# Three small reorderings in a fused attention and feed-forward kernel: batch 0's second chunk squared earlier, a matmul between two means, the last copy on two engines

## The chip, the cores and the metric

The kernel runs on one core of one Trainium2 chip. Times are device microseconds (us). Each profile is one execution; its span is 1.7 to 2.1 us shorter than the measured time of the same execution. Before the change the time was 284.89 us, the median of three runs (284.84 to 284.98).

## The reference

```python
def _attn_ref(q, k, v, g_norm):                    # (8, 8, 576, 64)
    kv = np.einsum('bhsd,bhse->bhde', k, v)
    out = np.einsum('bhsd,bhde->bhse', q, kv)
    rms = np.sqrt(np.mean(out * out, axis=-1, keepdims=True) + 1e-06)
    return out / rms * g_norm
# x = out, transposed to (4608 tokens, 512)
def _moe_ref(x, w_in, w_out):                      # 512 -> 2048 -> 512
    h = x @ w_in
    g = np.where(h > 0.0, h, np.exp(np.minimum(h, 0.0)) - 1.0)
    return g @ w_out
```

## The kernel before

Tokens are worked in tiles of 512. For the first tile, x is built in four chunks of 128 features (0, 2, 1, 3), and the first matmuls with `w_in` start as soon as a chunk is normalized. `idle` matmuls on zeros fill the start. The second tile (batch 1) is built in two groups, between the `mm2` matmuls (`o_ps`) of the first one. The parts that the change and the argument touch:

```python
def chunk_y(c, ps): ...            # y of chunk c: TensorE, 64-wide
def chunk_square(c):               # ScalarE
    nc.scalar.activation(sq0[c], y_ps[c], AF.Square)
def inv_t(r, ps):                  # ScalarE: Ln, then Exp(-0.5 *)
    nc.scalar.activation(r, ps, AF.Ln, bias=eps_col)
    nc.scalar.activation(r, r, AF.Exp, scale=-0.5)
# ... start of the kernel (cut) ...
    mean_mm(sq0[2], mean)
    inv_t(r[:, 1, :], mean)                     # chunk 2: Ln, Exp
    ...
    chunk_kv(kv_ps, 3)                          # needs chunk 3's v
    chunk_kv_out(kv_ps, 3, V)
    chunk_y(1, single("m", "y_ps"))
    chunk_square(1)
    ...
    chunk_y(3, y3)
    chunk_square(3)
    chunk_scale(2, r[:, 1, :])
    early([(0, 0), (0, 1)], 0)                  # matmuls of chunk 0
    mean_mm(sq0[1], mean)
    nc.scalar.activation(r[:, 0, :], mean, AF.Ln, bias=eps_col)
# ... a group of tile 1 (cut) ...
        for l in range(2):
            n.sums(l, single("m", "mean"))      # one mean matmul
            n.inv(l); n.scale(l)                # ScalarE, VectorE
        mm2_all(*((7, 11), (13, 15))[u])
# ... the last 128 tokens, 256 columns at a time (cut) ...
        for n, eng in enumerate((A, V)):        # ScalarE, then VectorE
            ...
            copy_on(eng, o, ps)
            last_store(J - 1, o, cols)
```

Of the kernel before, what the change touches and what calls it, by code (L numbers as in the profile page):

```python
# [10 lines left out]
AF = mybir.ActivationFunctionType  # L11
# [5 lines left out]
def kernel(  # L17
# [13 lines left out]
    nc = tc.nc  # L31
    P = 128

    B, H, S, D = q.shape
# [8 lines left out]
    V, A, Q = nc.vector, nc.scalar, nc.gpsimd  # L43
# [20 lines left out]
    eps_col = const.tile([P, 1], FP32, name="eps_col")  # L64
# [43 lines left out]
    def copy_on(eng, out_, in_):  # L108
        if eng is nc.scalar:
            nc.scalar.copy(out_, in_)  # L110
        else:
            eng.tensor_copy(out=out_, in_=in_)  # L112
# [16 lines left out]
    def single(tag, name):  # L129
        pool = ps_x if tag == "x" else ps_m2  # L130
        return pool.tile([P, 512], FP32, name=name, tag=tag)

    def pair(tag, name):
        if tag in ("x", "m", "mx"):
            return [single(t, name) for t in (tag + tag)[:2]]
        return ps_m1.tile([P, 2, 512], FP32, name=name, tag=tag)

    def as_bf16(ps):
        return ps.bitcast(BF16)
# [11 lines left out]
    def kv_mm(b, kv_ps, u, ls=range(2)):  # L151
        for j in range(RK):
            for s in range(2):
                rows = slice(s * 64, s * 64 + 64)
                for l in ls:
                    nc.tensor.matmul(  # L156
                        kv_ps[s][l * 64 : l * 64 + 64, u * 64 : u * 64 + 64],
                        lhsT=bf["k", b][rows, 2 * l + u, j, :],
                        rhs=bf["v", b][rows, 2 * l + u, j, :],
                        start=(j == 0),  # L160
                        stop=(j == RK - 1),
                    )

    def kv_out(b, kv_ps, u, engs):
        for s in range(2):
            copy_on(engs[s], kv_sb[:, b, u, s], kv_ps[s][:, u * 64 : u * 64 + 64])
# [11 lines left out]
    def q_t_out(b, u, eng, src, js):  # L178
        copy_on(eng, qT[b][:, :, u, js, :], src.rearrange("p (j s r) -> p s j r", s=2, r=64))

    def y_mm(T, u, ps, ls=range(2)):

        n = 0
        while n < 8:
            b, j = slot_of(T, n)
            m = min(8 - n, RK - j)
            for l in ls:
                for s in range(2):
                    nc.tensor.matmul(  # L189
                        ps[l][s * 64 : s * 64 + 64, n * 64 : (n + m) * 64],  # L190
                        lhsT=kv_of(b, l, u, s),
                        rhs=qT[b][l * 64 : l * 64 + 64, s, u, j : j + m, :],
                        start=True,
                        stop=True,
                    )
            n += m

    def mean_mm(sq, ps):
        nc.tensor.matmul(ps, lhsT=ones, rhs=sq, start=True, stop=True)  # L199
# [4 lines left out]
    def r_tile():  # L204
        return outp.tile([P, 2, G], FP32, name="rT", tag="o")

    def inv_t(r, ps):
        nc.scalar.activation(r, ps, AF.Ln, bias=eps_col)
        nc.scalar.activation(r, r, AF.Exp, scale=-0.5)  # L209

    def scale_t(T, ps, r, cs, cols=slice(0, 512)):
        nc.vector.scalar_tensor_tensor(  # L212
            out=xT[T][:, cs, cols], in0=ps, scalar=g_col, in1=r, op0=ALU.mult, op1=ALU.mult
        )
# [208 lines left out]
    def last_store(j, o, cols):  # L423
        rows = out_dram.rearrange("(b p j) f -> b p j f", b=B, j=RK)
        for h, eng in enumerate((nc.scalar, nc.sync)):
            b, jj = slot_of(NT - 1, 2 * j + h)
            eng.dma_start(out=rows[b][:, jj, cols], in_=o[h * 64 : h * 64 + 64])
# [5 lines left out]

    def last_columns():

        for n, eng in enumerate((A, V)):
            cols = slice(n * 256, n * 256 + 256)
            ps = single("m", "o_ps")[:, 0:256]
            for f in range(FC):
                nc.tensor.matmul(  # L440
                    ps,
                    lhsT=gT[NT - 1][:, f, (J - 1) * P : J * P],
                    rhs=w_out_sb[:, f, cols],
                    start=(f == 0),
                    stop=(f == FC - 1),
                )
            o = outp.tile([P, 2, DM], FP32, name="o_sb", tag="o")[:, 0, 0:256]
            copy_on(eng, o, ps)
            last_store(J - 1, o, cols)

    def mm2_half(T, i):
# [71 lines left out]
    def idle(n, ps):  # L523
        for _ in range(n):
            nc.tensor.matmul(ps, lhsT=zeros[:, 0:P], rhs=zeros, start=True, stop=True)

    def turned_q(b, u, tag):

        ps = as_bf16(single(tag, "qt_ps"))
        q_t_mm(b, u, range(8), ps)  # L530
        return ps
# [4 lines left out]
    def chunk_kv(kv_ps, c):  # L536
        kv_mm(0, [kv_ps[:, s, :] for s in range(2)], c % 2, (c // 2,))

    def chunk_kv_out(kv_ps, c, eng):
        rows, cols = slice(c // 2 * 64, c // 2 * 64 + 64), slice(c % 2 * 64, c % 2 * 64 + 64)  # L540
        copy_on(eng, kv_sb[rows, 0, c % 2], kv_ps[rows, :, cols])

    y_ps, sq0 = {}, {}

    def chunk_y(c, ps):
        y_ps[c] = ps
        y_mm(0, c % 2, {c // 2: ps}, (c // 2,))

    def chunk_square(c):
        sq0[c] = attp.tile([P, G], BF16, name="sq", tag="sq")  # L550
        nc.scalar.activation(sq0[c], y_ps[c], AF.Square)

    def chunk_scale(c, r, cols=slice(0, 512)):
        scale_t(0, y_ps[c][:, cols], r[:, cols], c, cols)
# [10 lines left out]
    def early(tiles, c):  # L565

        for i, a in tiles:
            h = h_ps[i]
            nc.tensor.matmul(  # L569
                h[a] if isinstance(h, list) else h[:, a, :],  # L570
                lhsT=w_in_sb[:, c, (2 * i + a) * P : (2 * i + a) * P + P],
                rhs=xT[0][:, c, :],
                start=(c == 0),
                stop=(c == KC - 1),
            )
# [10 lines left out]
    ps = turned_q(0, 0, "m")  # L586
# [5 lines left out]
    mean = pair("A", "mean")[:, 0, :]  # L592
# [10 lines left out]
    mean_mm(sq0[0], mean)  # L603
    r = r_tile()
    inv_t(r[:, 0, :], mean)
    mean = single("m", "mean")
    ps = turned_q(0, 1, "m")
    q_t_out(0, 1, V, ps, slice(0, 8))
    mean_mm(sq0[2], mean)
    inv_t(r[:, 1, :], mean)  # L610
    kv_ps = pair("B", "kv_ps")
    h_ps = [pair("A", "h_ps")]
    chunk_kv(kv_ps, 1)
    chunk_kv_out(kv_ps, 1, V)
    idle(2, h_ps[0][:, 0, :])
    chunk_scale(0, r[:, 0, :])
    chunk_kv(kv_ps, 3)
    chunk_kv_out(kv_ps, 3, V)
    chunk_y(1, single("m", "y_ps"))
    chunk_square(1)  # L620
    idle(1, h_ps[0][:, 0, :])
    y3 = single("x", "y_ps")
    h_ps += [None, [single("x", "h_ps"), None]]
    chunk_y(3, y3)
    chunk_square(3)
    chunk_scale(2, r[:, 1, :])
    h_ps[1] = pair("B", "h_ps")
    early([(0, 0), (0, 1)], 0)
    mean = single("m", "mean")
    mean_mm(sq0[1], mean)  # L630
    r = r_tile()
    nc.scalar.activation(r[:, 0, :], mean, AF.Ln, bias=eps_col)
    early([(1, 0), (1, 1), (2, 0)], 0)
    for n in range(2):
        cols = slice(n * 256, n * 256 + 256)
# [20 lines left out]
    def mm2_all(f0, f1, js=range(4)):  # L656
        for f in range(f0, f1):
            for j in js:
                mm2(0, j, f, f + 1)

    for tag, j0 in (("A", 0), ("B", 2)):
        ps = pair(tag, "o_ps")
# [4 lines left out]
    for u in range(2):  # L667
        n = Turned(1, u)
        if u == 0:
            for js in ((0, 1), (2, 3)):  # L670
                mm2_all(0, 4, js)
        kv_ps = [single("x", "kv_ps") for _ in range(2)]
        kv_mm(1, kv_ps, u)
        kv_out(1, kv_ps, u, (A, A))
        main = turned_q(1, u, "m")
        q_t_out(1, u, V, main, slice(0, 8))
        ends = as_bf16(single("m", "qt_ps"))
        for t in range(2):
            q_t_mm(t, u, (8,), ends[:, t * P : t * P + P])
        for t in range(2):  # L680
            q_t_out(t, u, V, ends[:, t * P : t * P + P], slice(8, 9))
        mm2_all(*((4, 6), (11, 12))[u])
        n.product([single("x", "y_ps") for _ in range(2)])
        for l in range(2):
            n.square(l)
        mm2_all(*((6, 7), (12, 13))[u])
        for l in range(2):
            n.sums(l, single("m", "mean"))
            n.inv(l)
            n.scale(l)  # L690
        mm2_all(*((7, 11), (13, 15))[u])
    for js in ((2, 3), (0, 1)):
        for j in js:
            mm2(0, j, 15, 16, out=False)
# [29 lines left out]
    ps = pair("B", "h_ps")  # L724
# [13 lines left out]
    ps = pair("A", "o_ps")  # L738
# [30 lines left out]
    for T in range(2, NT):  # L769
        at, early, late = {}, {}, {}  # L770
        if T + 1 < NT:
# [12 lines left out]
            early = {2: ("sum0", "inv0"), 4: ("sum1", "inv1"), 5: ("gain0",), 7: ("gain1",)}  # L784
            late = {0: ("kv",), 1: ("se0",), 2: ("mul0",), 3: ("se1",), 4: ("mul1", "ahead")}
        if T == 2:
            early = {2: ("sum0", "inv0"), 5: ("sum1", "inv1", "mul1"), 6: ("gain0",), 7: ("gain1",)}
# [45 lines left out]
```

## Time and profile before

| | before |
|---|---|
| time, median of 3 | 284.89 us |
| span of the profile | 283.0 us |
| TensorE busy | 273.8 us, 97% |
| chain of waits: TensorE's share | 93% |
| last matmul's end to last copy's end | 0.52 us |

What this bounds, and the lines that carry it, are in the prediction. In the timeline, start and length come first, then engine, source line, operation, output and inputs, and in brackets the idle time ahead of the first instruction of the row with what ended it. This is GpSimd in the profile of before, at the first piece of work that waits for batch 4's q:

```profile
60.61 4.07 POOL L103 CAST q_bf<-st_q 128x384 bf16<-128x384 f32 x6 [5.40 <-DMA st_q<-in_q_dram]
```

The bracket says that GpSimd sat idle until that load had landed, so 60.6 is the landing. And this is VectorE some 8 us later, with the transposes of x by DMA that it waits for:

```profile
69.02 0.48 DVE L312 TENSOR_SCALAR xT<-xT,g_col 128x1024 bf16<-128x1024 bf16 x1
70.70 0.48 DVE L312 TENSOR_SCALAR xT<-xT,g_col 128x1024 bf16<-128x1024 bf16 x1 [1.20 <-DMA xT<-xs]
```

The second of these ended at 71.18. TensorE came to its first matmul on it at 71.30 and did not have to wait.

### The profile page before, as it was taken

To read this page: it belongs to the slowest core of one execution; us is meant where nothing else is said; L and a number is where in the kernel's file an instruction comes from. 1 tells how busy PE (TensorE), PEld (TensorE's weight loads), DVE (VectorE), ACT (ScalarE), POOL (GpSimd) and SP (SyncE) were. 2 spreads that over 40 slices of the span, in tenths; PEclk is the share of its full clock that TensorE was granted. 3 is DMA by queue.
4 is the path that set the end of the run, shared out by engine and by line. 5 is a ranking of instruction groups with operands and counts; after the bars stand their busy time and mean duration, and the time that the engine had idled before them with its cause. 6 is when DMAs were issued, how large, how long until landed. Compare 5 with 4: busy or idle time off the path is not lost.

```text
span 283.0 us, 5120 instructions
## 1 busy us (share of the span) xinstructions
PE 273.8 (97%) x2089; PEld 128.9 (46%) x2123; DVE 164.9 (58%) x222; ACT 141.6 (50%) x209; POOL 50.0 (18%) x89
## 2 busy tenths in 40 slices
PE   7799999999999999999999999999999999999994
PEld 3444444444544444444444444444444444444443
DVE  2549532867578647655775478537873786344600
ACT  3778359594667355425542555245533553333311
POOL 7743303341340033034003210000000000000000
PEclk9999999999999999999999999999999999999999
DMA  7999999999996979689528961602150235020222
GB/s 209 201 204 206 206 263 228 208 257 180 199 264 89 155 210 223 80 211 249 140 30 175 263 159 39 162 17 74 39 111 0 74 39 111 0 76 0 74 74 75
DMA packets 50571, 39.46 MB, mean 139 GB/s; under 512 B 30964, under 2 KB 44020, under 8 KB 50548
## 3 DMA queue, kind: packets, MB, share of 16 engines
q0 software_dynamic: 15008, 21.30, 37.6%
q1 hardware_dynamic: 35136, 17.31, 28.6%
q10 hardware_dynamic: 404, 0.53, 0.5%
q8 instruction: 16, 0.26, 0.4%
q14 instruction: 7, 0.06, 0.1%
HBM read 36.70 MB, written 9.44 MB: 163 GB/s over the span
## 4 chain that ended last, share of the span: by engine, by line
PE 93%; DMA 3%; POOL 1%; issue 1%; DVE 1%; ACT 0%; POOLq 0%; DVEq 0%
PE o_ps L403 43%; PE h_ps L382 42%; DMA v_bf<-in_v_dram 3%; PE at L250 2%; PE at L156 2%; PE h_ps L569 1%; PE o_ps L440 1%; POOL k_bf L90 1%; PE mean L199 0%; PE qt_ps L174 0%; PE kv_ps L156 0%; PE y_ps L189 0%; POOL v_bf L90 0%; DVE xT L212 0%; POOL q_bf L90 0%
## 5 line engine op out<-in xcount | busy, mean ns | idle before, releaser
L403 PE MATMUL o_ps<-w_out_sb,gT 128*128 128x512 bf16 x548 | 128.4, 379 | 0.7 <-issue 0.2
L382 PE MATMUL h_ps<-xT,w_in_sb 128*128 128x512 bf16 (+1 forms) x540 | 126.4, 376 | 1.0
L350 ACT ACTIVATE elu_e<-h_ps 128x1024 bf16<-128x1024 f32 (+1 forms) x79 | 74.1, 952 | 89.2 <-PE h_ps L382 78.4
L403 PEld LDWEIGHTS <-gT 128*128 128x128 bf16 x560 | 54.3, 98 | 65.9 <-issue 0.9
L366 DVE TENSOR_TENSOR gT<-elu_e,h_ps 128x1024 bf16<-128x1024 bf16 (+1 forms) x67 | 77.2, 1157 | 6.9 <-PE h_ps L382 0.5
L382 PEld LDWEIGHTS <-w_in_sb 128*128 128x128 bf16 x560 | 53.2, 98 | 61.1 <-issue 0.2
L362 DVE TENSOR_SCALAR elu_e<-elu_e 128x1024 bf16<-128x1024 bf16 x72 | 31.5, 437 | 64.5 <-ACT elu_e L350 64.4
L419 ACT COPY o_sb<-o_ps 128x512 f32<-128x512 f32 x32 | 18.4, 588 | 20.8 <-PE o_ps L403 20.1
L103 POOL CAST q_bf<-st_q 128x384 bf16<-128x384 f32 x36 | 18.5, 558 | 38.0 <-DMA st_q<-in_q_dram 32.9
L283 DVE TENSOR_REDUCE ss<-sq 128x16 f32<-128x1024 bf16 x14 | 17.1, 1218 | 6.5 <-ACT sq L277 6.5
L299 DVE TENSOR_TENSOR xs<-at,ss 128x1024 bf16<-128x1024 f32 x14 | 17.1, 1219 | 1.9 <-ACT ss L292 1.9
L277 ACT ACTIVATE sq<-at 128x1024 bf16<-128x1024 f32 x14 | 14.4, 1028 | 0.0
L212 DVE SCALAR_TENSOR_TENSOR xT<-y_ps,g_col,rT 128x512 bf16<-128x512 f32 (+1 forms) x10 | 6.2, 641 | 10.1 <-ACT rT L209 7.9
L339 POOL COPY gate<-qT 1x16 bf16<-1x16 bf16 x5 | 1.1, 217 | 58.9 <-DMA qT<-q_bf 58.9
L355 ACT ACTIVATE elu_h<-h_ps 128x1024 bf16<-128x1024 f32 (+1 forms) x12 | 9.3, 816 | 0.0
L156 PEld LDWEIGHTS <-k_bf 64*64 64x64 bf16 x576 | 6.4, 107 | 5.5 <-issue 5.5
L90 POOL DMA_DIRECT2D v_bf<-in_v_dram x11 | 7.8, 711 | 4.2 <-DMA w_in_sb<-in_moe_w_in_dram 2.1
L90 POOL DMA_DIRECT2D k_bf<-in_k_dram x11 | 7.7, 702 | 2.5 <-DMA w_in_sb<-in_moe_w_in_dram 1.7
L312 DVE TENSOR_SCALAR xT<-xT,g_col 128x1024 bf16<-128x1024 bf16 x14 | 6.7, 480 | 1.9 <-DMA xT<-xs 1.9
L366 DVE TENSOR_TENSOR gT<-elu_e,elu_h 128x1024 bf16<-128x1024 bf16 x9 | 6.6, 736 | 0.8
L250 PEld LDWEIGHTS <-qT 64*128 64x128 bf16 (+1 forms) x248 | 4.3, 97 | 6.1 <-issue 5.9
L112 DVE COPY o_sb<-o_ps 128x256 f32<-128x256 f32 x1 | 0.4, 425 | 11.1 <-PE o_ps L440 11.1
(57 smaller groups left out, 100.4 us busy)
## 6 DMA issues: line engine op xcount, KB each, us to landing
st_q<-in_q_dram POOLq DMA_DIRECT2D x6, 1152.0 KB, 8.0
out_dram<-o_sb SPq DMA_DIRECT2D x24, 256.0 KB, 3.4
k_bf<-in_k_dram POOLq DMA_DIRECT2D x6, 576.0 KB, 10.2
v_bf<-in_v_dram POOLq DMA_DIRECT2D x6, 576.0 KB, 12.4
out_dram<-o_sb SPq DMA_DIRECT2D x19, 128.0 KB, 2.4
w_out_sb<-in_moe_w_out_dram POOLq DMA_DIRECT2D x4, 512.0 KB, 15.5
w_in_sb<-in_moe_w_in_dram POOLq DMA_DIRECT2D x2, 512.0 KB, 10.7
q_bf<-in_q_dram POOLq DMA_DIRECT2D x3, 288.0 KB, 13.5
```

The source lines that it names most:

```text
L90: eng.dma_start(out=dst.rearrange("p m j d -> p m (j d)"), in_=in_[:, ms, :])
L103: nc.gpsimd.tensor_copy(out=bf["q", b][:, u, js], in_=raw[b][:, u::2, js, :].rearrange("p l j d -> p j l d"),)
L156: nc.tensor.matmul(kv_ps[s][l * 64 : l * 64 + 64, u * 64 : u * 64 + 64], lhsT=bf["k", b][rows, 2 * l + u, j, :], rhs=bf["v", b][rows, 2 * ...
L277: nc.scalar.activation(sq, st["se", h], AF.Square)
L283: nc.vector.reduce_sum(out=ss, in_=st.pop(("sq", h)).rearrange("p l (m e) -> p (l m) e", e=D), axis=AX.X,)
L299: nc.vector.tensor_tensor(out=st["xs"][:, 2 * h : 2 * h + 2, :].rearrange("p i (l m e) -> p l i m e", l=2, e=D), in0=se_ps.rearrange("p l ...
L350: nc.scalar.activation(e[:, lo:hi, :], h, AF.Exp)
L362: nc.vector.tensor_scalar(out=e, in0=e, scalar1=1.0, scalar2=1.0, op0=ALU.min, op1=ALU.subtract)
L366: nc.vector.tensor_tensor(out=gT[T][:, 2 * i + lo : 2 * i + hi, :], in0=e[:, lo:hi, :], in1=h, op=ALU.add if relu else ALU.max,)
L382: nc.tensor.matmul((ps[a] if isinstance(ps, list) else ps[:, a, :])[:, cols], lhsT=w_in_sb[:, c, f * P : f * P + P], rhs=xT[T][:, c, cols] ...
L403: nc.tensor.matmul(o_ps[T, j], lhsT=gT[T][:, f, j * P : j * P + P], rhs=w_out_sb[:, f, :], start=(f == 0), stop=(f == FC - 1),)
L419: nc.scalar.copy(o_sb[T, half][:, j % 2, :], o_ps[T, j])
```

## The change

The intent: chunk 1 of the first tile is ready earlier (part 1); no idle time stands between the two means of a group (part 2); each of two engines copies only half of the last 256 columns (part 3).

```diff
@@ part 1 @@
-    mean = single("m", "mean")
     ps = turned_q(0, 1, "m")
     q_t_out(0, 1, V, ps, slice(0, 8))
+    mean = single("m", "mean")
     mean_mm(sq0[2], mean)
-    inv_t(r[:, 1, :], mean)
+    nc.scalar.activation(r[:, 1, :], mean, AF.Ln, bias=eps_col)
 ...
     chunk_scale(0, r[:, 0, :])
+    chunk_y(1, single("m", "y_ps"))
+    chunk_square(1)
+    nc.scalar.activation(r[:, 1, :], r[:, 1, :], AF.Exp, scale=-0.5)
     chunk_kv(kv_ps, 3)
     chunk_kv_out(kv_ps, 3, V)
-    chunk_y(1, single("m", "y_ps"))
-    chunk_square(1)
 ...
     chunk_y(3, y3)
-    chunk_square(3)
     chunk_scale(2, r[:, 1, :])
-    h_ps[1] = pair("B", "h_ps")
-    early([(0, 0), (0, 1)], 0)
 ...  (mean and Ln of chunk 1)
+    chunk_square(3)
+    h_ps[1] = pair("B", "h_ps")
+    early([(0, 0), (0, 1)], 0)
@@ part 2 @@
+        f0, f1 = ((7, 11), (13, 15))[u]
         for l in range(2):
             n.sums(l, single("m", "mean"))
             n.inv(l)
             n.scale(l)
-        mm2_all(*((7, 11), (13, 15))[u])
+            mm2_all(f0, f0 + 1, ((0,), (1, 2, 3))[l])
+        mm2_all(f0 + 1, f1)
@@ part 3 @@
-            copy_on(eng, o, ps)
+            if n == 0:
+                nc.scalar.copy(o, ps)
+            else:
+                nc.scalar.copy(o[:, 0:128], ps[:, 0:128])
+                nc.vector.tensor_copy(out=o[:, 128:256], in_=ps[:, 128:256])
```

More of the change, by code (lines that the diff above doesn't have):

```diff
@@ L434, in last_columns @@
     def last_columns():
-        for n, eng in enumerate((A, V)):
+        for n in range(2):
             cols = slice(n * 256, n * 256 + 256)
```

## The prediction

> **What bounds the kernel now.** I read the page of the profile first, then the chain that ended last (whole, and piece by piece for the first 45 us), then the timeline in narrow windows around the three places that the diff touches, and the landings of the loads that feed them.
>
> From the page, the span, the busy shares and the chain by engine:
>
> ```profile
> span 283.0 us, 5120 instructions
> PE 273.8 (97%) x2089; PEld 128.9 (46%) x2123; DVE 164.9 (58%) x222; ACT 141.6 (50%) x209; POOL 50.0 (18%) x89
> PE 93%; DMA 3%; POOL 1%; issue 1%; DVE 1%; ACT 0%; POOLq 0%; DVEq 0%
> ```
>
> TensorE is the bound nearly everywhere, so only a gap on TensorE, or work before its first or after its last matmul, can be won. The measured time is 284.89 us, 1.9 over the span. The change touches gaps of tenths of a microsecond: everything below is in hundredths.
>
> **First place, 12 to 18 us.** The chain there, start and length in us:
>
> ```profile
> 4.96 7.08 DMA v_bf<-in_v_dram
> ...
> 12.69 0.30 DVE kv_sb L112
> ...
> 13.09 0.40 PE y_ps L189 x2
> 13.49 0.54 PE h_ps L569 x2
> 14.03 0.23 PE mean L199
> 14.26 0.02 issue
> 14.29 0.70 ACT rT L632
> ...
> 15.01 0.43 ACT rT L636
> ...
> 15.86 0.49 DVE xT L212
> ```
>
> Four chunks of x are normalized in the order 0, 2, 1, 3. The early matmuls use chunk 0, then 2, and wait for chunk 1: the last of chunk 2 starts at 15.81, a matmul takes a slot of 0.216, so TensorE is free at 16.03 and starts chunk 1 at 16.39. That gap is 0.36. Chunk 3 starts at 17.71, where it could have started at 17.68. After that TensorE runs without a gap for many microseconds, so **what counts is when chunk 3 is ready**, not the larger gap before it.
>
> **Second place, 34 to 47 us**, batch 1's two groups. The timeline of group 1 (start, length, engine):
>
> ```profile
> 42.32 1.04 PE L403 MATMUL o_ps<-w_out_sb,gT 128*128 128x512 bf16 x4
> 43.19 0.74 PE L199 MATMUL mean<-sq,ones 128*128 128x512 bf16 x2
> 43.77 0.38 PE L403 MATMUL o_ps<-w_out_sb,gT 128*128 128x512 bf16 x1
> 46.23 0.75 DVE L212 SCALAR_TENSOR_TENSOR xT<-y_ps,g_col,rT 128x512 bf16<-128x512 f32 x1 [0.49 <-ACT rT L209]
> 46.79 1.48 PE L382 MATMUL h_ps<-xT,w_in_sb 128*128 128x512 bf16 x6
> ```
>
> The two means start at 43.19 and 43.56, 0.365 apart where 0.216 would do: the second waits for ScalarE's second square (42.92 to 43.51). So 0.15 of TensorE time is lost; group 0 shows the same (35.79 and 36.16). But look at the last two lines. The last chunk of x for tile 1 is ready at 46.98, and TensorE, which arrives at 47.01, starts it at 47.04. **The ScalarE/VectorE chain from the first mean to that chunk (43.19 to 46.98) and TensorE's own work between are within 0.03 of each other.** A gap filled between them buys nothing unless the first mean itself moves.
>
> What can hold the first mean? The four o_ps matmuls ahead of it read the last quarter of w_out. Its load:
>
> ```profile
> 27.45 0.77 POOL L122 DMA_DIRECT2D w_out_sb<-in_moe_w_out_dram  x1 [0.73 <-DMA k_bf<-in_k_dram]
> DMA to landing us min/median/max: 14.7/14.7/14.7
> ```
>
> It lands at about 42.10 (27.45 + 14.7, rounded in the view), 0.22 before its first use at 42.32. The DMA engines are full here, so it will not land sooner.
>
> **Third place, the end**:
>
> ```profile
> 277.42 0.37 ACT L110 COPY o_sb<-o_ps 128x256 f32<-128x256 f32 x1 [1.16 <-PE o_ps L440]
> 279.22 0.42 DVE L112 COPY o_sb<-o_ps 128x256 f32<-128x256 f32 x1 [11.10 <-PE o_ps L440]
> 279.68 0.47 SPq L427 DMA_DIRECT2D out_dram<-o_sb  x1
> 279.68 0.50 ACTq L427 DMA_DIRECT2D out_dram<-o_sb  x1
> ```
>
> The last matmul ends at 279.13, VectorE copies 279.22 to 279.65, the two stores go out at 279.68. All of this is on the path to the end.
>
> [...] the built order of the changed kernel shows the dependency: VectorE's half waits for a ScalarE count that is exactly that of ScalarE's half, where before it waited for TensorE. **The two halves run one after the other.** [...] squares of 512 take 0.60, Ln with its bias 0.69, and two squares start 0.50 apart. [...] from a 128-wide matmul to a 64-wide weight load passes 0.31 instead of 0.216.
>
> **The change, part by part.**
>
> (1) Chunk 1 ahead of chunk 3. No instruction is added or removed. I rebuild the stretch with the durations above. The idle matmul before chunk 1's product starts at 11.57, so the product starts at 11.88 (mode change 0.31) and ends at 12.28; its square runs 12.32 to 12.92 (ScalarE waits 0.24 for it), and chunk 2's Exp 12.82 to 13.45. Chunk 3's v lands at 12.04 as before, its product starts at 13.03 to 13.09. The mean of chunk 1 follows at 13.37 instead of 13.87, since two h matmuls no longer stand before it; its Ln starts at 13.80 instead of 14.29. But chunk 3's square now stands between Ln and Exp: 14.39, and the Exp's first half starts at 14.89 instead of 15.01. Gain 0.12, passed on by the scale to chunk 1 (16.27). Chunk 3: its mean at 15.10, Ln at 15.52 instead of 15.63, its last half scaled by 17.55, first matmul at 17.60 instead of 17.71. **Sum: 0.11 won**, not 0.36, because ScalarE still does the same four instructions before chunk 1's Exp.
>
> (2) A matmul between the means. In group 0 the 0.15 is filled: TensorE reaches group 1 0.11 + 0.15 = 0.26 earlier. The w_out quarter's first use would be at 42.06, but it lands at 42.10, and a matmul released by another engine starts some 0.05 after it (16.33 to 16.39 above): 42.15. So 0.17 of the 0.26 survives. In group 1 TensorE fills the second 0.15, but then arrives at the last chunk of x at 46.69, and that chunk is ready 0.17 earlier than before, not 0.32: it waits till 46.87. **Sum of (1) and (2): 0.17 won**, and group 1's filled gap comes back as a wait of 0.17. If (1) gave nothing, (2) alone would give 0.15 or 0.16.
>
> (3) The shared copy. ScalarE starts some 0.04 after the last matmul (as at 277.42): 279.17. 128 columns cost 0.373 - 128/1.2 ns = 0.27: ends 279.43. VectorE starts 0.03 later (its usual distance from ScalarE, 46.20 to 46.23) and takes 0.425 - 128/0.96 ns = 0.29: ends 279.76, instead of 279.65. **0.11 lost.** The stores are unchanged.
>
> Sum: 284.89 - 0.17 + 0.11 = **284.83 us**.
>
> **Rivals.** (A) The filled gaps count in full: 0.11 + 0.15 + 0.15 = 0.41 won, 0.11 lost, 284.59. For it: TensorE is 97% busy. Against it: the last chunk's readiness within 0.03 of TensorE's arrival. (B) The halves of the copy overlap: 0.13 won at the end instead of 0.11 lost, 284.59 with my 0.17. For it: two engines, half the columns. Against it: the wait in the built order. (C) The reordered start loses: ScalarE's wait of 0.24 for chunk 1's product, or the square before the Exp, pushes chunk 3 out by 0.1 to 0.2. Then the group 1 gate still has slack to take it, 0.0 to 0.1 won in all, 284.9 to 285.0. (D) The w_out quarter lands later in a run: less won, 284.9.
>
> **Range and chances.** The runs of before lie within 0.14 of each other. A and B mark the low side and C and D the high side, neither likely beyond 0.25: range 284.60 to 285.05. Two per cent is 5.7 us, which no part comes near: faster 0.01, same 0.98, slower 0.01.
>
> **What would show it.** In the changed profile: chunk 3's early matmuls start near 17.60; group 0's means stand 0.43 apart with an o_ps matmul between and no gap; the first matmul with the last w_out quarter starts 0.1 to 0.2 earlier than 42.32, not 0.26; a new TensorE gap of some 0.17 stands before the fourth h_ps matmul of tile 1; at the end a ScalarE copy of 128x128, then, not beside it, a VectorE copy, and stores some 0.6 us after the last matmul instead of 0.55. The prediction is wrong if the stretch 10 to 18 us moves by more than 0.2 either way, if tile 1's fourth matmul moves by 0.3, or if the two copies overlap.

Three figures need what the profile of before measured beside them. The "mode change" is the step from a 128-wide matmul to a 64-wide weight load, 0.309 us (34.26 to 34.57). "Full" means that from 27.45 to 42.10 us the DMA engines were busy for 90% or more of each of 40 slices, at 228 GB/s; that the load will not land sooner was an estimate. And the columns a ns in part (3), 1.2 and 0.96, are what two lengths in that profile give: ScalarE's copies of `o_ps` took 0.588 us for 512 columns and 0.373 for 256, so 1.19 columns a ns, and VectorE's products of `y_ps` 0.748 and 0.480, so 0.96.

## The result, and the profile after

The changed kernel takes 285.20 us (285.00 to 285.85, six runs), against 284.94 (284.82 to 285.59, six runs) for the kernel before in the same rounds. A ratio is the mean time of one kernel's fast runs over that of the other's of the same rounds, so it is not quite the ratio of these medians: here 1.0007, with a 95% interval of 0.9993 to 1.0021. That is "the same", as predicted, but the median lies 0.15 above the predicted range.

From the page of the changed kernel, the span, the busy times and the chain's shares:

```profile
span 283.3 us, 5120 instructions
PE 274.8 (97%) x2089; PEld 129.5 (46%) x2123; DVE 164.3 (58%) x222; ACT 141.4 (50%) x210; POOL 49.9 (18%) x89
PE 96%; DVE 1%; issue 1%; ACT 1%
```

TensorE has the same matmuls and is busy 1.0 us longer. Of that, 0.67 shows in the timeline of TensorE's first microseconds, in the ten idle matmuls. First before, then after:

```profile
1.19 3.78 PE L525 MATMUL kv_ps<-zeros 128*128 128x512 bf16 x10 [1.19 <-DVE one L518]
```

```profile
1.19 4.45 PE L529 MATMUL kv_ps<-zeros 128*128 128x512 bf16 x10 [1.19 <-DVE one L522]
```

The same ten matmuls took 3.78 and 4.45 us. The profile's clock record of TensorE rises to full speed at 4.15 us in the one and at 6.73 in the other; below it a slot (from the start of one 512-column matmul to that of the next) is 0.427 us, above it 0.216. The change does not touch anything there. In the twenty profiles the rise lies between 4.15 and 7.17 us, 3.02 apart, in kernels whose starts differ at most by two idle matmuls and one memset of a single number. What sets the moment was not shown.

**The first place.** The chain of the changed kernel, start and length, at its beginning and at this stage:

```profile
1.19 4.44 PE kv_ps L529 x10
5.64 0.19 PE g_ps L586
```

```profile
13.79 0.34 PE mean L199
14.12 0.02 issue
14.15 0.69 ACT rT L634
14.83 0.49 ACT sq L555
15.32 0.32 ACT rT L641
15.63 0.02 issue
15.66 0.34 DVE xT L212
16.00 0.06 issue
16.06 0.48 DVE xT L212
16.55 0.04 issue
16.59 0.59 PE h_ps L573 x2
```

As predicted, chunk 3's square (L555) stands between chunk 1's Ln and Exp. But the chain now comes from the ten idle matmuls, where before it came from the load of v (the prediction shows it), and the first Ln starts at 10.58 instead of 10.16. Chunk 3's first matmul starts at 17.97, not at the predicted 17.60; before, it was 17.71.

**The second place.** The timeline of TensorE in group 1, and the chain right behind it:

```profile
42.43 1.04 PE L403 MATMUL o_ps<-w_out_sb,gT 128*128 128x512 bf16 x4
43.30 0.38 PE L199 MATMUL mean<-sq,ones 128*128 128x512 bf16 x1
43.52 0.38 PE L403 MATMUL o_ps<-w_out_sb,gT 128*128 128x512 bf16 x1
43.74 0.38 PE L199 MATMUL mean<-sq,ones 128*128 128x512 bf16 x1
```

```profile
46.49 0.65 PE h_ps L382 x3
47.14 0.01 issue
47.15 1.02 PE h_ps L382 x4
```

The gap between the means is filled: 43.30, 43.52, 43.74 are 0.216 apart. The fourth h_ps matmul comes 0.386 after the third (46.76 to 47.15) where a slot is 0.216: 0.17 of waiting, the size that the prediction gave. But the first matmul on the last quarter of w_out starts at 42.43, later than before (42.32), not earlier. The trace counts that quarter as landed at 42.23; before, at 42.10. In neither profile did the landing hold it: TensorE got there 0.20 and 0.22 after it. The 0.11 is chunk 3's delay of 0.26 less the 0.15 that was filled in group 0.

**The third place**, the end:

```profile
279.35 0.27 ACT L451 COPY o_sb<-o_ps 128x128 f32<-128x128 f32 x1 [1.38 <-PE o_ps L440]
279.64 0.29 DVE L452 COPY o_sb<-o_ps 128x128 f32<-128x128 f32 x1 [11.34 <-ACT o_sb L451]
279.96 0.47 SPq L427 DMA_DIRECT2D out_dram<-o_sb  x1
```

VectorE's half waits for ScalarE's half, as predicted. The last copy ends 0.626 after the last matmul, before 0.517: **0.109 lost, predicted 0.11**.

The difference of the spans (283.27 less 282.96, so 0.31) is then: 0.11 at the end of tile 1 (TensorE gets there at 52.97 instead of 52.86), 0.07 around 71 us (VectorE's second multiplication starts at 71.05 instead of 70.70), 0.11 at the end, and 0.02 in the closing instructions. Only the last but one is plainly the change. The experiments had to show whether any of the rest is.

### The profile page after: what moved, and what is told of

The parts are those of the page before. It is cut to its first block, busy times and chain, and to the rows that moved or that the text cites. A ratio compares the mean times of both kernels' runs of the same rounds, so it can differ in the third digit from the quotient of the medians.

```text
span 283.3 us, 5120 instructions
## 1 busy us (share of the span) xinstructions
PE 274.8 (97%) x2089; PEld 129.5 (46%) x2123; DVE 164.3 (58%) x222; ACT 141.4 (50%) x210; POOL 49.9 (18%) x89
## 4 chain that ended last, share of the span: by engine, by line
PE 96%; DVE 1%; issue 1%; ACT 1%
PE o_ps L403 43%; PE h_ps L382 42%; PE at L250 2%; PE kv_ps L529 2%; PE at L156 2%; PE o_ps L440 1%; PE h_ps L573 1%; PE qt_ps L174 1%; PE kv_ps L156 1%; PE mean L199 1%; PE y_ps L189 1%; DVE kv_sb L112 0%; DVE xT L212 0%; DVE qT L112 0%; ACT rT L634 0%
## 5 line engine op out<-in xcount | busy, mean ns | idle before, releaser
L350 ACT ACTIVATE elu_e<-h_ps 128x1024 bf16<-128x1024 f32 (+1 forms) x79 | 74.0, 952 | 89.4 <-PE h_ps L382 78.6
L362 DVE TENSOR_SCALAR elu_e<-elu_e 128x1024 bf16<-128x1024 bf16 x72 | 30.9, 430 | 65.0 <-ACT elu_e L350 64.8
```

The costliest lines, as they stand in the source:

```text
L350: nc.scalar.activation(e[:, lo:hi, :], h, AF.Exp)
L362: nc.vector.tensor_scalar(out=e, in0=e, scalar1=1.0, scalar2=1.0, op0=ALU.min, op1=ALU.subtract)
```

## The experiments

Eighteen runs followed (three of them repeats of a kernel), each with five rounds against the kernel before on the same chip. All gave correct results. The table keeps what they are about; the columns are explained below it.

| run | order of chunks | clock rise | chunk 3 | w_out landing | end of tile 1 | q cast | 53 to 76 | tail |
|---|---|---|---|---|---|---|---|---|
| before | old | 4.15 | 17.71 | 42.10 | 52.86 (+10.76) | 60.61 | 23.26 | 0.517 |
| before2 | old | 5.53 | 17.78 | 42.50 | 53.07 (+10.57) | 61.03 | 23.38 | 0.518 |
| idle8 | old | 6.05 | 17.77 | 42.26 | 52.93 (+10.67) | 60.84 | 23.34 | 0.518 |
| act_b | old | 5.57 | 17.81 | 42.32 | 53.00 (+10.68) | 61.69 | 23.91 | 0.409 |
| p3 | old | 6.86 | 17.89 | 42.25 | 53.03 (+10.78) | 60.73 | 23.26 | 0.626 |
| bm1 | old | 6.98 | 17.87 | 42.44 | 53.02 (+10.59) | 62.95 | 24.73 | 0.887 |
| p2 | old | 6.44 | 17.82 | 42.32 | 52.89 (+10.57) | 61.82 | 23.83 | 0.516 |
| p1 | new | 4.21 | 17.84 | 42.38 | 52.99 (+10.61) | 61.50 | 23.29 | 0.871 |
| p1b | new | 6.29 | 17.77 | 42.38 | 53.00 (+10.62) | 61.93 | 23.93 | 0.871 |
| p1v | new | 5.78 | 17.86 | 42.22 | 53.02 (+10.79) | 60.62 | 23.48 | 0.517 |
| after | new | 6.73 | 17.97 | 42.23 | 52.97 (+10.74) | 61.33 | 23.33 | 0.626 |
| after2 | new | 6.00 | 17.67 | 42.27 | 52.84 (+10.57) | 61.66 | 23.76 | 0.627 |
| p12 | new | 5.74 | 17.90 | 42.45 | 53.02 (+10.58) | 62.07 | 23.84 | 0.870 |
| p12v | new | 5.65 | 17.91 | 42.34 | 52.92 (+10.58) | 61.11 | 23.26 | 0.518 |
| gates | new | 7.17 | 17.97 | 42.37 | 52.80 (+10.43) | 61.73 | 23.26 | 0.626 |
| open2 | new | 5.02 | 17.63 | 42.28 | 52.68 (+10.40) | 61.78 | 23.73 | 0.627 |
| best8 | third | 4.16 | 17.80 | 42.35 | 52.75 (+10.40) | 61.95 | 23.66 | 0.409 |
| best | third | 6.53 | 17.67 | 42.27 | 52.66 (+10.40) | 61.19 | 23.81 | 0.411 |
| best2 | third | 4.53 | 17.62 | 42.32 | 52.72 (+10.40) | 61.73 | 23.92 | 0.409 |
| best3 | old | 4.18 | 17.64 | 42.24 | 52.64 (+10.40) | 61.80 | 23.97 | 0.410 |

The rows before and after are the two first profiles. Times are us from the span's start. "Third" is the new order with chunk 3's square ahead of chunk 1's Ln and its mean two matmuls earlier. "Chunk 3" is the start of the first tile's first matmul on it. The landing, of w_out's last quarter, is read from the trace's counts of finished transfers. "End of tile 1" is the start of the last weight load ahead of the pause of 0.52 in which TensorE changes to the 64-wide matmuls with k near 53 us, with its distance from that landing in parentheses. "q cast" is the start of GpSimd's cast, which follows the landing of batch 4's q. "53 to 76" runs from that end of tile 1 to the next pause of that kind near 76 us (with q). "Tail" is from the end of the last matmul to the end of the last copy. From the mark at 76 us to the end of the last matmul it takes 203.01 or 203.02 us in 18 of the 20 profiles (in gates and best8 203.77, because they move matmuls there). **So whatever two kernels differ by has happened by 76 us, or after the last matmul.**

### 1. The parts apart, and the changed kernel again

`p1`, `p2` and `p3` hold one part of the diff above each; `after2` is the changed kernel unaltered. What the expectations call the clock's phase is only the moment at which it rose in a profile (4.15 us in before, 6.73 in after), and their warm-up matmuls are the idle ones; that these bring the rise about was not shown.

```diff
 p1: before + the hunks of part 1 only
 p2: before + the hunk of part 2 only
 p3: before + the hunk of part 3 only
 after2: before + all hunks
```

> Part 1 alone: the early chunks reordered, everything else as before. Theory 1 (the clock's phase made the difference): the first tile's chunk-3 matmul stands 0.11 to 0.17 us nearer to the first Ln than in the kernel before (7.56 us after it there), and the median is 0.0 to 0.2 us below that of the kernel before of the same rounds; how late the whole start is depends only on which of the ten warm-up matmuls is the first to run at a slot of 0.216 us. Rival (the reorder itself costs time at the start): the median is 0.2 to 0.3 us above.

> Part 2 alone: a matmul between the two means of each group. Theory: both means stand 0.43 us apart with no gap, and before the fourth h_ps matmul of tile 1 a step of 0.36 to 0.39 us appears instead of 0.24, so that of the 0.30 us filled only the 0.15 us of group 0 survives; median 0.10 to 0.17 us below the kernel before. Rival (the filled gaps count in full): no new step, 0.30 us below.

> Part 3 alone: the last copy shared. Theory: VectorE's half starts 0.03 us after ScalarE's half has ended, from the end of the last matmul to the end of the copies pass 0.63 us instead of 0.52, and the median is 0.11 us above the kernel before. Rival (the halves run side by side): 0.38 us from matmul to the end of the copies, 0.13 us below.

> The changed kernel unaltered, for more samples. Theory 1 (clock phase): the runs again spread over 0.5 us or more, and so do those of the kernel before in the same rounds; in the profile the number of slow warm-up matmuls (slot 0.427 us) need not be ten as in the first profile. Rival: the first profile's late start is a property of the changed kernel, ten slow warm-up matmuls again, and its lowest time stays 0.15 us above that of the kernel before.

Against a kernel before of 285.21 (284.75 to 286.88, eleven runs):

| | median | lowest to highest | ratio, 95% interval |
|---|---|---|---|
| p1 | 285.40 | 285.16 to 286.90 | 1.0004, 0.9976 to 1.0033 |
| p2 | 285.27 | 284.73 to 286.59 | 1.0004, 0.9971 to 1.0037 |
| p3 | 285.13 | 284.95 to 285.43 | 0.9988, 0.9963 to 1.0012 |
| after2 | 285.54 | 285.07 to 286.86 | 1.0006, 0.9978 to 1.0034 |

No median tells the parts apart, and those expected of p1, p2 and p3 were missed. The kernel before itself spreads over 2.1 us here, where its first three runs lay within 0.14. What the profiles do tell:

Part 1. In p3, in the old order, chunk 3's first matmul stands 7.28 us after the first Ln; in the changed kernel's two profiles 7.39. The changed order is 0.11 slower when nothing else holds it, because ScalarE waits twice in it (0.24 us for chunk 1's product, as the prediction had it, and 0.28 for its mean) and once in the old one (0.15). The third order removes the second of these waits and stands at 7.17. The changed order had looked 0.11 to 0.17 faster against the one profile of before, where the distance was 7.55: there the early clock had put the first Ln at 10.16, and chunk 3's v, which landed at 12.04, held the old order. In p1's profile (first Ln at 10.07) that is gone, but a slab of w_in (the part that one load brings) landed at 16.49 and held chunk 1, so the distance was 7.77. This start is a race between TensorE's clock and the loads, and the order of the chunks decides only which load is felt.

Part 2. Both gaps are filled, and the step behind them is the predicted wait in all five profiles with part 2 and an unaltered tile 1. Part 3 costs 0.109 on its own too (tail 0.626).

Part 1's fastest run is 285.16, and its tail is 0.871: VectorE's last copy starts 0.446 after the last matmul and not 0.09. That was unexplained until experiment 4.

The table shows what holds the end of tile 1. Without part 2 it comes 35.15 to 35.23 after chunk 3's first matmul in eight of nine profiles; in the ninth, before2, w_out's last quarter landed latest and holds it. Part 2 takes 0.15 off TensorE's way (35.00 in after), and then that landing holds it in four of five: the end of tile 1 follows it by 10.57 or 10.58.

### 2. The start, the copy and the two waits by themselves

```diff
 idle8:  -    idle(10, kv_ps[:, 0, :])
         +    idle(8, kv_ps[:, 0, :])
 act_b:  -        for n, eng in enumerate((A, V)):
         +        for n, eng in enumerate((A, A)):
 gates (changed kernel, and):
         -        mm1_part(T, i, ps, range(KC))
         +        if (T, i) == (1, 0):
         +            mm1_part(T, i, ps, range(KC - 1), last=False)
         +            mm1_part(T, i, ps, (KC - 1,))
         +        else:
         +            mm1_part(T, i, ps, range(KC))
         ...
         +            mm2_half(T - 1, 5)   # tile 2: after the first column half of h_ps
 best8:  gates + idle(8) + act_b's copy + chunk 3's square ahead of chunk 1's Ln
         and chunk 3's mean two matmuls earlier
```

> The kernel before with 8 warm-up matmuls ahead of the first transposes instead of 10. Theory 1 (the clock's phase): in six profiles so far the first Ln starts at 10.07 to 10.16 us where the clock rose at 4.2 us, and at 10.28, 10.47, 10.58 and 10.61 where it rose at 6.0, 6.4, 6.7 and 6.9, whatever the kernel; late runs pay because ten slow matmuls (0.427 us each) block TensorE till 5.4. With eight they end at 4.6, so the first transpose starts at 5.4 even in a late run, and the first Ln by about 10.3 even there. Median 0.0 to 0.3 us below the kernel before, more where most runs are late. Rival (the start is set by the loads, or fewer warm-up matmuls delay the clock): Ln as late as before or later.

> The kernel before with the whole last copy on ScalarE in place of VectorE: 0.04 us after the last matmul and 0.37 us long, so 0.41 us from matmul to the end of the copy, where VectorE alone took 0.52 and the shared copy 0.63. Median 0.11 us below the kernel before, if the spread of the start lets it be seen. Rival (the end is set by something else than this copy): the last store is issued as late as before.

> The changed kernel with its two later waits given slack: tile 1's chunk-3 matmuls of the first pair stand last (three more matmuls ahead), and one half of an o_ps group stands between the two column halves of tile 2's first pair (eight more matmuls ahead). Theory: the step of 0.39 us at 47 us falls to 0.22, the one at 71.4 us (0.07, 0.47 and 0.42 us in three profiles with part 2) to none; median 0.2 to 0.6 us below the changed kernel. Rival (the time is given back at yet another wait): both steps gone, and a new one behind them.

> All together: parts 1 and 2, chunk 3 squared ahead of chunk 1's Ln and its mean two matmuls earlier, the two waits with slack, the last copy on ScalarE alone, 8 warm-up matmuls. Theory: chunk 3's first matmul comes another 0.15 us earlier after the first Ln than in the changed kernel (7.39), no step at 47 and 71 us, 0.41 us from the last matmul to the end of the copy; median 0.4 to 0.8 us below the kernel before. Rival: the gains at the start are held back by the landing of the last w_out quarter at 42.1 to 42.4 us, and only 0.3 to 0.4 us remain.

Against a kernel before of 285.62 (284.85 to 286.98, eleven runs) the four medians were 285.12, 285.66, 285.54 and 285.67, and all four intervals of the ratio hold 1 (idle8 0.9991, act_b 0.9991, gates 0.9995, best8 1.0007).

idle8 runs two idle matmuls less at the start, and its first Ln came at 10.03 although its clock rose late (6.05; in best8, also with eight, 4.16); the end of tile 1 did not follow (52.93), because a slab of w_in landed at 16.42 and held chunk 1. Its median lies 0.50 below the kernel before, where 0.0 to 0.3 was expected; the interval (0.9957 to 1.0025) does not tell this from chance. act_b shortens the tail, in the profile by 0.11:

```profile
279.96 0.37 ACT L110 COPY o_sb<-o_ps 128x256 f32<-128x256 f32 x1 [1.37 <-PE o_ps L440]
```

ScalarE alone starts 0.037 after the last matmul and takes 0.372, in all 0.409, against 0.517 on VectorE alone and 0.626 shared. The tail's saving is plain in the profile and invisible in the median.

gates took both waits away, at 47 and at 71 us, and paid for it with a new gap at 78.6 us (0.97 from one matmul to the next, 0.76 over a slot), since the half of `o_ps` that it moved forward had been the filler there. best8 did the same (0.64 over a slot). Those two were my design errors, not measurements of a limit, and both missed their expected medians.

### 3. Both waits taken away otherwise, and two repeats

```diff
 open2 (changed kernel, gates' first edit, and):
         -            opened = [pair("B", "h_ps")]
         -            mm1_part(T, 0, opened[0], range(KC), slice(0, 256))
         +            opened = [pair(t, "h_ps") for t in "BA"]
         +            for i in range(2):
         +                mm1_part(T, i, opened[i], range(KC), slice(0, 256))
 best:   open2 + act_b's copy + the third order of chunks, as in best8
 before2: the kernel before    p1b: p1
```

> The changed kernel with two waits taken away otherwise than in the run called gates: in tile 1's first pair of h_ps the chunk-3 matmuls of the first tile go last, and in tile 2 the first column halves of both h_ps pairs stand ahead of both second halves. Theory (small gaps can be won, if nothing else fills them): tile 1's step at 47 us falls from 0.39 to 0.22, no TensorE gap over 0.1 at 70 to 73 us whenever the transposes land up to 0.6 us late, none near 79 us (the run called gates had 0.97 there); the median is 0.2 to 0.5 below a run of the changed kernel, 284.7 to 285.0 where the clock rises by 5 us. Rival (what is won before the last w_out quarter or a transpose lands is given back at the next landing, and the spread of the runs is larger): a median within 0.2 of the kernel before, ratio's interval holding 1.

> All that the profiles say could be won, in one kernel: chunk 3's square ahead of chunk 2's Exp, part 2 of the change, both waits taken away as in open2, and the last copies on ScalarE alone. Theory: chunk 3's first matmul stands 7.1 to 7.2 after the first Ln (7.39 in the changed order, 7.28 in the old one) unless a w_in slab lands later; no steps at 47 and 71 us; the last copy ends 0.41 after the last matmul instead of 0.52 (before) and 0.63 (changed); median 0.3 to 0.6 below the kernel before. Rival: the last w_out quarter lands at 42.2 to 42.4 as elsewhere and holds the front, so only the tail's 0.11 is won, and the interval of the ratio holds 1.

> The kernel before once more, as a run of its own. Theory: nothing distinguishes it from the kernel before but the moment its clock rises and its landings; its median is within 0.3 of the kernel before of the same rounds, its runs spread over 0.3 or more (the prediction took 0.14). In its profile chunk 3's first matmul stands 7.28 after the first Ln, as in the other three profiles of the old order in which the v load did not hold it, against 7.39 in the changed order; tile 1's fourth h_ps matmul at 47.0 to 47.2; the last copy ends 0.52 after the last matmul. Rival (the first profile of before is what the kernel is): 7.55, and runs within 0.14.

> Part 1 of the change alone, once more. Two things were odd in its first run: its fastest time was 285.16 where the others' were near 284.8, and VectorE's last copy started 0.45 after the last matmul instead of 0.09. Theory (chance): the copy starts 0.09 after the last matmul, the fastest run is below 285.0, chunk 3's first matmul stands 7.39 after the first Ln unless a w_in slab lands after it. Rival (the reordered start does something later on): fastest run again above 285.1, and the late copy again.

(The expectations of best and best2 put chunk 3's square "ahead of chunk 2's Exp"; the edit has it behind that and ahead of chunk 1's Ln.) The same runs of before served as in experiment 2, with one more. Medians: open2 285.63 (1.0003, 0.9973 to 1.0034), best 285.11 (0.9983, 0.9955 to 1.0011), p1b 285.63 (0.9993, 0.9963 to 1.0023). before2, which is the kernel before under another name, has 285.03 and a ratio of 0.9975 with an interval of 0.9949 to 1.0001. **A kernel compared with itself thus came out 0.25% faster, with an interval that barely holds 1.** Effects of 0.1 us, 0.035% of the time, cannot be had from such medians, and the expectation that before2 would lie within 0.3 of before was a miss.

In before2 the distance of chunk 3 from the first Ln was 7.42, where 7.28 was expected. Its first Ln is at 10.36 and its v landed at 12.07, 1.71 later. In before that is 1.88 (distance 7.55), in p3 1.39 and in act_b 1.56 (distance 7.28 in both). So the old order is held by the v load when the first Ln comes early. That agrees with the reading of part 1, though not with its expected number.

best has the front 0.20 ahead of before at the end of tile 1, and a tail of 0.41, and yet no shorter span. In it and in open2, opening the second pair early made TensorE wait for the buffer:

```profile
70.57 0.02 issue
70.59 1.08 ACT o_sb L423 x2
71.68 0.04 issue
71.72 1.36 PE h_ps L382 x11
```

This is best's chain: TensorE stands until two ScalarE copies have emptied the PSUM pair that it is to fill. From one matmul to the next pass 0.56 where a slot of 256 columns is 0.11: 0.45 was given back. The steps at 47 us were gone as expected, in best chunk 3 stood 7.17 after the first Ln and the tail was 0.41, but the gap at 71 us was a miss, and so was open2's median. That of best is 0.52 below the kernel before, within its expected 0.3 to 0.6; but before2, which changes nothing, lies 0.60 below.

p1b gave the late copy again, to the nanosecond: 0.446 after the last matmul.

### 4. The late copy: VectorE's 320th record

Part 1 changes nothing at the end of the kernel. But the built order shows that it spares VectorE one wait early on, so that VectorE has 324 records in the trace instead of 325 (waits counted). In every profile where it can be seen, VectorE's 320th record starts 0.40 to 0.45 us after the 319th ended; neighbours that wait for nothing follow within 0.05. In the kernel before, that record is the last wait ahead of the last copy, and the pause is over long before TensorE is done. With one record less, the 320th **is** the last copy. The next experiments set the number of records without touching anything else.

```diff
 p1v  (p1, and):   nc.vector.memset(one, 1.0)
              +    nc.vector.memset(one, 1.0)          # a second time
 bm1  (before): -    nc.vector.memset(one, 1.0)
              +    nc.gpsimd.memset(one, 1.0)
 p12:  before + parts 1 and 2        p12v: p12 + the second memset
```

> Part 1 alone, with one more VectorE instruction at the start (the 1x1 constant is filled twice), so that VectorE again has 325 records as in the kernel before and not 324. Theory (VectorE's 320th record always starts 0.40 after the end of the one before instead of 0.05; part 1 saves VectorE one wait instruction and so moves that pause from the last wait, where it is hidden, onto the last copy): the last copy starts 0.09 after the last matmul instead of 0.45, and the fastest run falls by 0.35, to 284.8 to 284.9 (285.16 and 285.21 in part 1's two runs). Rival (the late copy comes from the reordered start in some other way, a store landing for one): 0.45 again and a fastest run near 285.2.

> The kernel before with one VectorE instruction less (GpSimd fills the 1x1 constant); the order on TensorE and ScalarE is unchanged, the order of the chunks is the old one. Theory of VectorE's 320th record: the last copy starts 0.45 after the last matmul, the last copy ends 0.87 after it instead of 0.52, and the fastest run is 285.1 to 285.2 (before 284.75 to 284.85). Rival (it is the reordered start): copy 0.09 after the last matmul, fastest run 284.8.

> Parts 1 and 2 without the shared copy. Theory: VectorE has 324 records, so the last copy starts 0.45 after the last matmul and ends 0.87 after it; fastest run 285.2 to 285.4, so that taking part 3 out of the changed kernel makes it slower by some 0.2 (its tail is 0.63), although part 3 alone costs 0.11. Rival: tail 0.52 and 0.1 below the changed kernel.

> Parts 1 and 2 without the shared copy, with the one more VectorE instruction. Theory: tail 0.52; fastest run 284.8 to 285.0, 0.35 below the run without that instruction; tile 1's fourth matmul still waits (step 0.39 or so) and stands at 47.0 to 47.15; from the end of that stretch at 76 us to the last matmul 203.01 as in all other runs. Rival (parts 1 and 2 win what was predicted, 0.17, in every run): fastest run 284.6 to 284.7.

The last copies, from the timelines of p1b, of p1v and of bm1:

```profile
280.39 0.42 DVE L112 COPY o_sb<-o_ps 128x256 f32<-128x256 f32 x1 [11.45 <-DMA out_dram<-o_sb]
```

```profile
279.61 0.42 DVE L112 COPY o_sb<-o_ps 128x256 f32<-128x256 f32 x1 [11.10 <-PE o_ps L440]
```

```profile
281.23 0.42 DVE L112 COPY o_sb<-o_ps 128x256 f32<-128x256 f32 x1 [11.47 <-DMA out_dram<-o_sb]
```

Those copies start 0.446, 0.092 and 0.463 after their last matmul. The memset that was added to part 1 took the delay away, and the memset that was removed from the kernel before, whose order of chunks is the old one, brought it in. The name in the bracket misleads: the "DMA out_dram" is only the last wait that the profile could put a name to, long met by then. The tails of p12 and p12v are 0.870 and 0.518. All four expected tails were met.

What goes with the pause shows in the transfers by queue. In the kernel before, from 275 to 279 us, and in p1, from 279 to 283 us, there is one packet of this kind each, and none in the other of the two windows:

```profile
q14 instruction: 1, 0.01, 0.8%
```

```profile
q14 instruction: 1, 0.01, 0.5%
```

An instruction fetch of 8 KB starts 0.66 after the 320th record in before (276.59 against 275.93) and 0.93 after it in p1 (280.67 against 279.74), and it moves with that record in every kernel (with the 319th where the 320th is VectorE's half of the shared copy). Fetches on this queue also begin 0.9 to 1.2 us after VectorE's 64th and 1.2 to 1.5 after its 192nd record in all twenty profiles, and the 192nd has the same pause (0.40 to 0.42 in the nine profiles where it can be seen). The three records are 128 apart. That the pause belongs to the fetching of VectorE's instructions is an inference from this and was not shown. The 320th record starts 0.40 after the end of the one before instead of 0.05, and this is hidden only while the engine waits anyway. In the changed kernel it is hidden as well (the fetch is at 276.88), because there the 320th record is VectorE's half of the copy, which waits for ScalarE anyway.

In the times: against a kernel before of 285.05 (284.94 to 286.10, eleven runs), p1v has 285.04 (five runs, lowest 285.01; ratio 0.9994, 0.9980 to 1.0008), bm1 286.13 (285.35; 1.0035, 1.0014 to 1.0056), p12 285.82 (285.40; 1.0032, 1.0010 to 1.0055) and p12v 285.47 (284.81; 1.0011, 0.9990 to 1.0032). The two with the late copy are the first whose interval excludes 1, but their ratios amount to 0.9 to 1.0 us, more than the 0.35 to 0.37 of their tails, so the cost of the pause is read from the profiles and not from the times. bm1's lowest run missed the expectation by 0.15; its profile shows a wait of 1.37 at 71.6 us besides. p1v's lowest run missed the expected 284.8 to 284.9 by 0.1.

So **the parts do not add up**. Part 3 alone costs 0.11. But taken out of the changed kernel it leaves p12, whose tail is 0.24 longer, not 0.11 shorter.

### 5. What lasts

```diff
 best2: best without the edit to tile 2 (opened stays as it was)
 best3: before + part 2 + gates' first edit + act_b's copy   (old order of chunks)
```

> What the runs so far say is won without being given back: chunk 3's square ahead of chunk 2's Exp, part 2, chunk 3's matmuls last in tile 1's first pair, the last copies on ScalarE alone, and tile 2 left as it was (both ways of reordering it lost 0.3 to 0.9 at 71 to 79 us). Theory: no step at 47 us; the end of tile 1 stands 10.4 after the last w_out quarter's landing (10.57 where the step was left in), so near 52.7; the stretch from there to 76 us takes 23.3, or 23.7 and more where a transpose lands late; then 203.01 to the last matmul; the copy ends 0.41 after it. Fastest run 284.4 to 284.6, the median 0.2 to 0.5 below the kernel before. Rival (what is won at 53 us is given back by the transposes in most runs): fastest run 284.7 or more, interval of the ratio holding 1.

> The same with the old order of the chunks, so without part 1 in any form. Theory (the last w_out quarter's landing sets the front behind it, and the order of the chunks is absorbed there): the end of tile 1 again 10.4 after that landing, tail 0.41, fastest run and median within 0.2 of best2. Rival (the order of the chunks counts): 0.2 or more above best2, with the front at 53 us later by as much at the same landing.

Both did what was expected up to 53 us: no step at 47, the end of tile 1 exactly 10.40 after the w_out landing, and a tail of 0.41. The order of the chunks made no difference at that mark: 10.40 in both. The times were a miss: best2 286.30 (285.19 to 287.00; ratio 1.0045, 1.0027 to 1.0062) and best3 285.40 (284.69 to 286.85; 1.0017, 0.9998 to 1.0036) against 285.03 (284.82 to 285.85, eleven runs). The gain went at 71 us. best2's chain there:

```profile
66.94 0.70 DVE gT L366
67.65 0.10 SPq L306
67.75 0.04 issue
67.79 3.51 DMA xT<-xs
71.30 0.03 issue
71.33 0.02 DVEq L312
71.35 0.05 issue
71.40 0.50 DVE xT L312
71.90 0.04 issue
71.94 1.03 PE h_ps L382 x8
```

The transposes of x were issued earlier than before (the second at 67.79, before at 68.12), and landed later: 3.51 us to landing here. From that issue to VectorE's use of it passed 3.61 us here, 2.58 in before and 4.43 in bm1, the run with the latest cast of q (62.95). What else differs stands in GpSimd's timeline of best2, in the same line that was shown of before:

```profile
61.73 2.16 POOL L103 CAST q_bf<-st_q 128x384 bf16<-128x384 f32 x3 [6.67 <-DMA st_q<-in_q_dram]
```

Batch 4's q landed 1.1 later, and the v behind it at 68.24 instead of 66.58, so that these loads still ran beside the transposes (from 68 to 70 us the DMA engines moved 325 GB/s in best2 and 163 in before). The table shows the two together all through; no run moved these loads on purpose. In the eight profiles with tile 2 unaltered and the cast at 61.50 or earlier, the stretch from 53 to 76 us took 23.26 to 23.48; in the eight with the cast at 61.66 or later, 23.76 to 24.73. Where the load is late, being earlier with the transposes wins nothing: in act_b, p2, after2 and best2 VectorE's second multiplication starts at 71.56, 71.34, 71.29 and 71.40, although their ends of tile 1 lie 0.28 apart.

No kernel here beats the kernel before with an interval that excludes 1. best3 has the fastest single run of all (284.69), but not the median.

## Why the prediction was right or wrong

**The step that failed is "Sum of (1) and (2): 0.17 won".** In the changed kernel's profile tile 1 ended 0.11 later instead of 0.17 earlier. The first Ln came 0.42 later, behind ten idle matmuls that ran till 5.64 instead of 4.97; the new order gave 0.17 of this back and group 0's filled gap 0.15. By the prediction's own sign, "moves by more than 0.2", the first place was wrong: chunk 3 came 0.26 later. Over all profiles the 0.17 shrinks to 0.06, as follows.

**Class: right.** Nothing came near two per cent, and TensorE's bound was read correctly.

**Step 3, the shared copy: right.** ScalarE's half took 0.265 and VectorE's 0.292, one after the other, and the tail grew by 0.109. The rival that the halves overlap (B) fell; the wait that was read from the built order is in the profile.

**Step 2, the matmul between the means: mechanism right, size wrong.** Both gaps were filled, and group 1's came back as a wait of 0.17 at the place named. What failed is "So 0.17 of the 0.26 survives". It was worked out with w_out's last quarter landing at 42.10, and that is the earliest landing of all twenty profiles; the others have 42.22 to 42.50. With tile 1 as it was, four of the five profiles with part 2 end tile 1 at 10.57 or 10.58 behind that landing, so they are bound by it; at 42.10 that would be 52.68, 0.18 ahead of before's 52.86, just the predicted gain. On average over the profiles, the end of tile 1 is at 52.99 without part 2 (nine profiles) and at 52.93 with it (five): 0.06 and not 0.17, where single profiles of either kind lie up to 0.2 apart. Rival D, "the w_out quarter lands later", is what four of the five show, and had been given too little weight; in the fifth, the changed kernel's first, the late start held instead. The "0.17 of wait" that part 2 leaves is real: the six kernels that reorder tile 1's first pair end 10.40 to 10.43 behind the landing.

**Step 1, the order of the chunks: wrong as a property of the change.** The rebuilt path itself was nearly right: it puts chunk 3 at 17.60, 7.44 after a first Ln at 10.16, and 7.39 was measured. But "Sum: 0.11 won" held for the conditions of one profile, an early clock and a v load that held the old order. The undisturbed distance from the first Ln to chunk 3 is 7.28 in the old order and 7.39 in the new one, so 0.11 are lost, which is what rival C said. The changed kernel's profile had the late clock (first Ln at 10.58), which gave 10.58 + 7.39 = 17.97. Behind it the start counts in full up to the end of tile 1, unless w_out's landing comes later still.

**Not in the prediction at all:** the stretch around 71 us, which takes 0.2 or 0.6 or 1.5 us more or less by the landing of batch 4's loads, and the pause of 0.40 at VectorE's 320th record, which part 1 moves by one instruction. The latter is harmless in the changed kernel only thanks to part 3.

**The range: wrong.** "The runs of before lie within 0.14 of each other" was taken for the spread of the measurement. Over all rounds the kernel before ran from 284.75 to 286.98, and before2 shows a ratio of 0.9975 against itself. The profile of before was moreover a lucky one: earliest clock, earliest w_out landing, q cast before 61 us. Every gap was priced against it.

**The account of the 0.31 in span.** Of the profiled difference, 0.109 is the change (part 3). The 0.11 at the end of tile 1 is its late clock, less what the new order and part 2 gave back; w_out's landing did not hold it (10.57 behind that would be 52.80, and it was 52.97). The 0.07 at 71 us is a transpose that landed late; after2 has neither in that size (52.84, but 23.76). Whether the changed kernel is truly slower than before by one or two tenths is not settled: both of its ratios (1.0007 and 1.0006) hold 1, and only the tail's 0.11 was there in every profile that has part 3.

**What stays open.** Why batch 4's q lands at 60.6 in one run and at 61.7 in the next, issued at 52.5 to 53.0 in both; p1 and p1b, which are the same kernel, fell on either side. Why best2's other five runs lay up to 1.8 above its profiled one, which was its fastest; no profile shows them. And what VectorE does in the pause: the fetch that goes with it starts only after the record, so the trace shows where the pause falls, and not what it waits for.

## What to carry to other kernels

Before pricing tenths of a microsecond, take several profiles of the kernel before and look for what differs between them: the moment the clock rises, and the landing that ends each wait; a gain that ends at a landing is worth only what the usual landing leaves. Count an engine's instructions as well as their times: sparing one wait moved a pause of 0.4 us onto the last copy and cost more than any part was to win. And a reordering early on can be taken back 20 us later by a transfer that nobody moved, so follow a change to the last point at which the two traces still differ.
